# Softplus as one ScalarE function, and a shorter join of float64 words, in an attention and two-MLP kernel

## Chip, cores and metric

The kernel runs on one core of one Trainium2 chip. The metric is the device time of one execution in microseconds (us). TensorE (PE in the profile; PEld is its weight load), VectorE (DVE), ScalarE (ACT), GpSimd (POOL) and the DMA queue that SyncE issues (SP) work beside each other, and each goes through its own instructions in order.

## The reference

Linear attention without softmax, with an RMS norm of each head, feeds an MLP with softplus, and that feeds a second MLP whose hidden layer is the largest of three products:

```python
kv  = einsum('bhsd,bhse->bhde', k, v)              # 8 batches, 8 heads, 576 x 64
o   = einsum('bhsd,bhde->bhse', q, kv)
x   = o / sqrt(mean(o*o) + 1e-6) * g_norm          # 4608 tokens x 512
h   = x @ w_in                                     # 512 x 2048
g   = maximum(h, 0) + log1p(exp(-abs(h)))          # softplus
x   = g @ w_out                                    # 2048 x 512
h   = maximum(maximum(x @ w1, x @ w2), x @ w3)     # 512 x 768 each
out = h @ w_out2                                   # 768 x 512
```

The weights arrive as float64: each is two 32-bit words, which the kernel joins into one float32.

## The kernel before, in words

**Passes.** Features lie on the 128 partitions, tokens run along the free dimension. The 4608 tokens go through in five passes (`NS`): two columns of 464 tokens at a time in passes 0 to 3, two of 448 in pass 4. In every pass the products of the MLPs are 2 x 2 block products by a scheme of seven multiplications: `product` (L309) makes one of seven (`ORDER`), a weight group has seven, and `sums` (L338) collects their results from PSUM: ACT copies (L111) take some out, DVE adds (L120) the others. Groups H0 to H7 make h, X00 to X31 make the second x, then nine groups and an output stage make the second MLP.

**Pass 0** multiplies in float32 (L318), and meanwhile makes the weights. `load_raw` (L209) loads 128 x 512 float64 words into one of two `raw` buffers; `to_f32` (L214) joins them into `sw`, through one PSUM buffer, `cv`: ACT takes the absolute value of the high word (L220), and four DVE operations follow (a lower limit L221, shift and mask L222, sign and top bit L226, the low word's three bits L231). There are two such conversions for each of 25 groups, and six for the output stage, 56 in all. Then POOL makes four sums of a group's weights (`sums_of_weights`, L123 and L120 on POOL), and `make_unit` splits them into a high and a low part for the other passes (ACT cast L111, POOL subtraction L117 into `u`) and writes them to DRAM (`wd`, L165). All of these loads and writes go through SP's one queue.

**Passes 1 to 4** load those parts (`u`, `ux`) and make three fp32r multiplications for each float32 one (`mm3`, L127 to L129). The attention of the next pass runs beside the second MLP of the present one (`attention_beside`).

**The functions touched.** `softplus` (L370) takes one tile of h, 128 x 464: ACT makes |h| (L372), exp (L373), ln (L374), and DVE adds max(h, 0) (L375). A pass has 32 of these, the run 160. `norm` (L499) makes the RMS factor: ACT takes ln (L503), exp (L504) and square (L505), two DVE operations follow (L506, L509), and DVE (L514, pass 0) or POOL (L519) scales the attention's output. There are 40 of these, eight a pass; those of pass 0 come before the first H group. ln, exp and the simple functions stand in one table set, loaded once at the start (L744).

**What sets the order.** Every step of the program is put on a list with a due time (`at`), the list is sorted, and the framework's scheduler then sets each engine's order when the program is built. So a change in a step's operations can move other instructions too.

Of the kernel before, what the change touches and what calls it, by code (L numbers as in the profile page):

```python
# [7 lines left out]
F32 = mybir.dt.float32  # L8
F32R = mybir.dt.float32r
I32 = mybir.dt.int32  # L10
AF = mybir.ActivationFunctionType
ALU = mybir.AluOpType

B, H, S, D = 8, 8, 576, 64
# [11 lines left out]
EPS = 1e-06  # L26

# [13 lines left out]
def kernel(  # L41
# [12 lines left out]
    nc = tc.nc  # L54
# [45 lines left out]
    epsc = const.tile([P, 1], F32, name="epsc")  # L100
# [31 lines left out]
    turns = {}  # L132

    def turn(key, *engs):
        k = turns[key] = turns.get(key, -1) + 1
        return engs[k % len(engs)]
# [16 lines left out]
    wd, units, st = {}, {}, {}  # L153
# [60 lines left out]
    def to_f32(raw, dst):  # L214

        t = psum("cv", "cv")
        lo32, hi32, u = raw[:, :, 0], raw[:, :, 1], t.bitcast(I32)
        nc.scalar.activation(t, hi32.bitcast(F32), AF.Abs)  # L220
        nc.vector.tensor_scalar_max(t, t, 2.0**-15)  # L221
        nc.vector.tensor_scalar(  # L222
            out=u, in0=u, scalar1=3, scalar2=0x3FFFFFF8,
            op0=ALU.logical_shift_left, op1=ALU.bitwise_and,
        )
        nc.vector.scalar_tensor_tensor(  # L226
            out=u, in0=hi32, scalar=-0x40000000, in1=u, op0=ALU.bitwise_and, op1=ALU.bitwise_or
        )
        r = len(dst.shape) - 1
        lo32, u = ((lo32, u) if r == 1 else (a.rearrange("p (i n) -> p i n", i=2) for a in (lo32, u)))  # L230
        nc.vector.scalar_tensor_tensor(  # L231
            out=dst.bitcast(I32), in0=lo32, scalar=29, in1=u,
            op0=ALU.logical_shift_right, op1=ALU.bitwise_or,
        )
# [135 lines left out]
    def softplus(p, src):  # L370
        e = ge_tile(p, "e", src.shape[1])
        nc.scalar.activation(e, src, AF.Abs)  # L372
        nc.scalar.activation(e, e, AF.Exp, scale=-1.0)  # L373
        nc.scalar.activation(e, e, AF.Ln, bias=1.0)  # L374
        nc.vector.scalar_tensor_tensor(  # L375
            out=e, in0=src, scalar=0.0, in1=e, op0=ALU.max, op1=ALU.add
        )
        return e
# [120 lines left out]
    def norm(a, n, p):  # L499

        ss = ss_t.pop((a, p))
        r, t = ctile("r", n), ctile("t", n)
        nc.scalar.activation(r, ss, AF.Ln, scale=1.0 / D, bias=epsc)  # L503
        nc.scalar.activation(r, r, AF.Exp, scale=-0.5)  # L504
# [239 lines left out]
    nc.scalar.preload_act_table_set("natural_log_exp_and_others")  # L744
# [11 lines left out]
    t = -60  # L756
# [103 lines left out]
```

## Time and profile before

| | |
|---|---|
| median of 3 runs | 1477.41 us (1475.75 to 1478.09) |
| profiled execution | span 1475.5 us, first to last instruction; the runs' times stand 0.3 to 2.6 us above it |
| PE busy | 1419.6 us (96%) |
| PEld busy | 1126.5 us (76%) |
| DVE busy | 933.5 us (63%) |
| ACT busy | 835.7 us (57%) |
| POOL busy | 676.5 us (46%) |

Busy is the time with at least one instruction in work; a share over the whole span is an average over stages with different limits. A matmul's end is modelled, and in passes 1 to 4 each overlaps the next, so a short gap between two starts does not show as idle PE; the number of matmuls or weight loads that start in a stretch (the x after a busy time) shows it. Pass 0 with the first attention lasts from 0 to about 400 us, each other pass about 270 us.

### The profile page before, as it was taken

How to read it: one execution, taken by the hardware profiler on the slowest of the kernel's cores; microseconds unless marked ns; L12 is line 12 of the kernel's file. 1: busy time of each engine (PE TensorE's matmuls, PEld its weight loads, DVE VectorE, ACT ScalarE, POOL GpSimd, SP SyncE). 2: the span in 40 equal slices, each digit the busy share in tenths (PEclk: the TensorE clock that was granted, in tenths of full speed). 3: DMA queues.
4: the chain of work that ended last, by engine and by line, in shares of the span. 5: the costliest groups of instructions: out<-in, count | busy, mean ns of one | idle time of the engine just before them, and what ended most of it. 6: DMA issues, size and time to landing. Idle time of an engine off the chain costs nothing.

```text
span 1475.5 us, 18888 instructions
## 1 busy us (share of the span) xinstructions
PE 1419.6 (96%) x6164; PEld 1126.5 (76%) x6164; DVE 933.5 (63%) x1476; ACT 835.7 (57%) x1625; POOL 676.5 (46%) x613
## 2 busy tenths in 40 slices
PE   6799998999999999999999999999999999999999
PEld 4344444555588889788888898888888888998998
DVE  5787888789366676773666656355675545567341
ACT  5676453554187636764866455387636637863321
POOL 3587777633234453451545434433454452445211
PEclk9999999999999999999999999999999999999999
DMA  7758667964366676766566776566676656666562
GB/s 273 251 185 274 214 221 271 337 215 157 110 203 203 217 236 224 266 236 214 190 213 215 247 252 202 167 201 213 212 221 193 215 172 208 206 209 213 183 220 96
DMA packets 107953, 315.56 MB, mean 214 GB/s; under 512 B 12112, under 2 KB 23632, under 8 KB 107856
## 3 DMA queue, kind: packets, MB, share of 16 engines
q1 hardware_dynamic: 107856, 314.36, 65.0%
q8 instruction: 50, 0.82, 0.2%
q14 instruction: 47, 0.39, 0.1%
HBM read 248.78 MB, written 65.54 MB: 213 GB/s over the span
## 4 chain that ended last, share of the span: by engine, by line
PE 74%; DVE 8%; ACT 6%; POOL 4%; issue 4%; DMA 3%; SPq 0%; POOLq 0%; ACTq 0%; DVEq 0%
PE Xx L127 3%; PE Xo L128 3%; PE Xx L129 3%; PE Xx L128 3%; PE Xo L129 3%; PE Xo L127 3%; PE Xh L127 3%; PE Xh L129 3%; PE Xh L128 3%; PE Xo L318 3%; PE oacc L697 3%; PE oacc L128 2%; PE oacc L129 2%; PE oacc L127 2%; PE kvps L412 2%
## 5 line engine op out<-in xcount | busy, mean ns | idle before, releaser
L117 POOL TENSOR_TENSOR lo<-e,hi 128x464 fp32r<-128x464 f32 (+1 forms) x160 | 190.6, 1225 | 197.6 <-ACT hi L111 151.9
L123 POOL TENSOR_TENSOR e<-e 128x464 f32<-128x464 f32 (+1 forms) x40 | 48.2, 1206 | 189.9 <-DVE t L123 164.9
L111 ACT COPY m<-Xo 128x464 f32<-128x464 f32 (+1 forms) x135 | 72.7, 543 | 88.6 <-PE Xo L129 73.7
L111 ACT CAST hi<-t 128x464 fp32r<-128x464 f32 (+1 forms) x96 | 52.1, 544 | 105.0 <-DVE t L123 44.2
L117 POOL TENSOR_TENSOR hl<-m,hh 128x464 fp32r<-128x464 f32 (+1 forms) x48 | 59.0, 1232 | 104.6 <-ACT hh L111 104.6
L375 DVE SCALAR_TENSOR_TENSOR e<-h,e 128x464 f32<-128x464 f32 (+1 forms) x80 | 68.0, 853 | 46.1 <-ACT e L374 45.7
L111 ACT CAST hi<-e 128x464 fp32r<-128x464 f32 (+1 forms) x160 | 87.0, 576 | 16.1 <-PE Yx L128 14.0
L374 ACT ACTIVATE e<-e 128x464 f32<-128x464 f32 (+1 forms) x160 | 92.8, 587 | 2.7
L373 ACT ACTIVATE e<-e 128x464 f32<-128x464 f32 (+1 forms) x160 | 92.9, 588 | 2.4
L120 DVE TENSOR_TENSOR x<-x,Xx 128x464 f32<-128x464 f32 (+1 forms) x120 | 75.3, 628 | 28.3 <-PE Xx L129 26.2
L117 POOL TENSOR_TENSOR u<-sw,u 128x512 fp32r<-128x512 f32 (+1 forms) x76 | 88.2, 1188 | 8.5 <-ACT u L111 8.4
L127 PE MATMUL Xo<-hi,u 128*128 128x464 f32 (+1 forms) x228 | 86.5, 379 | 1.4 <-ACT m L111 1.4
L123 POOL TENSOR_TENSOR sw<-sw 128x256 f32<-128x256 f32 x75 | 57.3, 764 | 65.9 <-DVE sw L231 44.9
L129 PE MATMUL Xo<-hi,u 128*128 128x464 f32 (+1 forms) x228 | 85.0, 373 | 0.0
L128 PE MATMUL Xo<-lo,u 128*128 128x464 f32 (+1 forms) x228 | 85.0, 373 | 0.0
L220 ACT ACTIVATE cv<-raw 128x512 f32<-128x512 f32 x56 | 35.9, 641 | 84.7 <-DVE sw L231 43.6
L519 POOL TENSOR_TENSOR og<-og,r 128x464 f32<-128x464 f32 (+1 forms) x32 | 41.0, 1280 | 88.7 <-DVE r L509 84.3
L127 PE MATMUL Xh<-hi,u 128*128 128x464 f32 (+1 forms) x194 | 73.4, 378 | 4.7 <-ACT h L111 4.3
L129 PE MATMUL Xh<-hi,u 128*128 128x464 f32 (+1 forms) x194 | 71.9, 371 | 0.0
L111 ACT COPY h<-Xh 128x464 f32<-128x464 f32 (+1 forms) x108 | 57.7, 536 | 24.9 <-PE Xh L129 21.4
L128 PE MATMUL Xh<-lo,u 128*128 128x464 f32 (+1 forms) x194 | 71.8, 370 | 0.0
L127 PE MATMUL Xx<-hi,u 128*128 128x464 f32 (+1 forms) x192 | 71.7, 374 | 0.0
(229 smaller groups left out, 4326.7 us busy)
## 6 DMA issues: line engine op xcount, KB each, us to landing
u<-wd SPq DMA_DIRECT2D x198, 512.0 KB, 4.4
ux<-wd SPq DMA_DIRECT2D x96, 512.0 KB, 3.4
wd<-u SPq DMA_DIRECT2D x79, 512.0 KB, 3.1
u<-wd SPq DMA_DIRECT2D x106, 256.0 KB, 3.8
raw<-in_w_out_dram SPq DMA_DIRECT2D x22, 512.0 KB, 4.2
k<-in_kp_dram SPq DMA_DIRECT2D x32, 320.0 KB, 4.9
v<-in_vp_dram SPq DMA_DIRECT2D x32, 320.0 KB, 5.3
raw<-in_w_dram SPq DMA_DIRECT2D x18, 512.0 KB, 4.2
```

The costliest lines, as they stand in the source:

```text
L111: nc.scalar.copy(hi, src)
L117: eng_lo.tensor_tensor(out=lo, in0=src, in1=hi.bitcast(F32), op=ALU.subtract)
L120: eng.tensor_tensor(out=o, in0=a, in1=b, op=ALU.add)
L123: eng.tensor_tensor(out=o, in0=a, in1=b, op=ALU.subtract)
L127: nc.tensor.matmul(acc, wh, xh, start=first, stop=False, skip_group_check=on)
L128: nc.tensor.matmul(acc, wh, xl, start=False, stop=False, skip_group_check=on)
L129: nc.tensor.matmul(acc, wl, xh, start=False, stop=last, skip_group_check=on)
L318: nc.tensor.matmul(acc, w[:, c * P:(c + 1) * P], rhs[m, c], start=first and c == 0, stop=c == 1, skip_group_check=not first)
L373: nc.scalar.activation(e, e, AF.Exp, scale=-1.0)
L374: nc.scalar.activation(e, e, AF.Ln, bias=1.0)
L375: nc.vector.scalar_tensor_tensor(out=e, in0=src, scalar=0.0, in1=e, op0=ALU.max, op1=ALU.add)
L697: nc.tensor.matmul(acc[e, t], w[:, o * P:(o + 1) * P], hh[f, t], start=f == 0, stop=f == NF2 - 1)
```

## The change

Three edits:

- `softplus` is one ACT operation, with the function Softplus. The two other ACT operations and the DVE operation go.
- Softplus is in another table set than ln and exp. `with_table` loads a set when the next function needs another than the last one, and ties the order: a load is issued after all activations that used the set before, an activation after its load. The load at the start goes; the first norm loads its set.
- `to_f32` joins the words with two ACT and two DVE operations. ACT scales the high word, read as float32, by 2^-112 into `cv`, and turns the low word into an integer of its three top bits, in place in `raw`. DVE shifts and joins the two, and then sets the sign from the high word.

```diff
+SLACK = 2.0**-16
+LOW_SCALE = 2.0**-29 * (1 - SLACK)
+LOW_BIAS = -0.5 + 7.5 * SLACK
+NORM_SET, PLUS_SET = "natural_log_exp_and_others", "softplus"
...
+    tables = {"set": None, "load": None, "used": []}
+
+    def after(ins):
+        st = ExitStack()
+        for i in ins:
+            st.enter_context(tc.issue_after(i))
+        return st
+
+    def with_table(name, out, src, func, **kw):
+
+        if tables["set"] != name:
+            with after(tables["used"]):
+                load = nc.scalar.preload_act_table_set(name)
+            tables.update(set=name, load=load.ins, used=[])
+        with after([tables["load"]]):
+            tables["used"].append(nc.scalar.activation(out, src, func, **kw).ins)
...
         lo32, hi32, u = raw[:, :, 0], raw[:, :, 1], t.bitcast(I32)
-        nc.scalar.activation(t, hi32.bitcast(F32), AF.Abs)
-        nc.vector.tensor_scalar_max(t, t, 2.0**-15)
-        nc.vector.tensor_scalar(
-            out=u, in0=u, scalar1=3, scalar2=0x3FFFFFF8,
-            op0=ALU.logical_shift_left, op1=ALU.bitwise_and,
-        )
+        nc.scalar.activation(t, hi32.bitcast(F32), AF.Copy, scale=2.0**-112)
+        nc.scalar.activation(lo32, lo32.bitcast(U32), AF.Copy, scale=LOW_SCALE, bias=LOW_BIAS)
         nc.vector.scalar_tensor_tensor(
-            out=u, in0=hi32, scalar=-0x40000000, in1=u, op0=ALU.bitwise_and, op1=ALU.bitwise_or
+            out=u, in0=u, scalar=3, in1=lo32, op0=ALU.logical_shift_left, op1=ALU.bitwise_or
         )
...
         nc.vector.scalar_tensor_tensor(
-            out=dst.bitcast(I32), in0=lo32, scalar=29, in1=u,
-            op0=ALU.logical_shift_right, op1=ALU.bitwise_or,
+            out=dst.bitcast(I32), in0=hi32, scalar=-0x80000000, in1=u,
+            op0=ALU.bitwise_and, op1=ALU.bitwise_or,
         )
...
     def softplus(p, src):
         e = ge_tile(p, "e", src.shape[1])
-        nc.scalar.activation(e, src, AF.Abs)
-        nc.scalar.activation(e, e, AF.Exp, scale=-1.0)
-        nc.scalar.activation(e, e, AF.Ln, bias=1.0)
-        nc.vector.scalar_tensor_tensor(
-            out=e, in0=src, scalar=0.0, in1=e, op0=ALU.max, op1=ALU.add
-        )
+        with_table(PLUS_SET, e, src, AF.Softplus)
         return e
...
-        nc.scalar.activation(r, ss, AF.Ln, scale=1.0 / D, bias=epsc)
-        nc.scalar.activation(r, r, AF.Exp, scale=-0.5)
+        with_table(NORM_SET, r, ss, AF.Ln, scale=1.0 / D, bias=epsc)
+        with_table(NORM_SET, r, r, AF.Exp, scale=-0.5)
...
-    nc.scalar.preload_act_table_set("natural_log_exp_and_others")
```

The built program has ten table loads where there was one: one at ACT's start, as before, one after the last norm before each pass's softplus (five), and one after the last softplus of each pass but the fifth (four).

ACT at the end of pass 0's attention: the last norm's instructions and the first H group's (`r`, `t` are the norm's tiles, `h11` an evicted product, `e` a softplus), before:

```order
L503 ACTIVATE r_339<-ss_337,epsc_82 128x464
L504 ACTIVATE r_339<-r_339 128x464
L505 ACTIVATE t_340<-r_339 128x464
L220 ACTIVATE cv_477<-raw_411 128x512
L111 COPY h11_400<-Xh_397 128x464
L372 ACTIVATE e_435<-Wh_431 128x464
L373 ACTIVATE e_435<-e_435 128x464
L374 ACTIVATE e_435<-e_435 128x464
```

The same place with the change:

```order
L152 ACTIVATE r_339<-ss_337,epsc_82 128x464
L152 ACTIVATE r_339<-r_339 128x464
L149 ACT_TABLE_LOAD
L512 ACTIVATE t_340<-r_339 128x464
L116 COPY h11_397<-Xh_394 128x464
L236 ACTIVATE cv_517<-raw_445 128x512
L237 ACTIVATE raw_445<-raw_445 128x512
L152 ACTIVATE e_431<-Wh_427 128x464
```

The table load stands between the norm's exp and its square, and the first softplus is one instruction.

ACT in pass 2, where H2 and H3 are evicted and the first four tiles of g are split for X00 (`CAST hi`), before:

```order
L111 COPY h22_5839<-Xh_5742 128x464
L111 CAST hi_5713<-e_5619 128x464
L372 ACTIVATE e_5828<-Wh_5820 128x464
L111 CAST hi_5717<-e_5690 128x464
L373 ACTIVATE e_5828<-e_5828 128x464
L111 CAST hi_5721<-e_5532 128x464
L374 ACTIVATE e_5828<-e_5828 128x464
L111 CAST hi_5725<-e_5575 128x464
L372 ACTIVATE e_5842<-h22_5839 128x464
L373 ACTIVATE e_5842<-e_5842 128x464
L374 ACTIVATE e_5842<-e_5842 128x464
L111 COPY h11_5854<-Xh_5847 128x464
```

The same place with the change:

```order
L116 CAST hi_5464<-e_5329 128x464
L152 ACTIVATE e_5561<-Wh_5553 128x464
L116 CAST hi_5519<-e_5406 128x464
L116 COPY h22_5569<-Xh_5478 128x464
L116 CAST hi_5523<-t1_5525 128x464
L116 COPY h11_5581<-Xh_5574 128x464
L152 ACTIVATE e_5572<-h22_5569 128x464
```

The eviction of H3's first product (`h11`) has one softplus operation between itself and the eviction of H2's last (`h22`) where it had six.

SP's queue in pass 0, where the eleventh to fourteenth load of raw words stand among the writes of the fourth and fifth group's parts (`wd12` to `wd19`), before:

```order
L165 DMA wd13_684<-u_681 128x1024
L211 DMA raw_637<-in_w_out_dram 128x1024
L165 DMA wd14_700<-u_697 128x1024
L165 DMA wd15_714<-u3_711 128x512
L211 DMA raw_675<-in_w_out_dram 128x1024
L165 DMA wd16_753<-u_750 128x1024
L211 DMA raw_731<-in_w_in_dram 128x1024
L165 DMA wd17_778<-u_775 128x1024
L165 DMA wd18_794<-u_791 128x1024
L211 DMA raw_769<-in_w_in_dram 128x1024
L165 DMA wd19_803<-u3_800 128x512
```

The same place with the change:

```order
L181 DMA wd14_658<-u_655 128x1024
L181 DMA wd15_669<-u3_666 128x512
L227 DMA raw_602<-in_w_out_dram 128x1024
L227 DMA raw_636<-in_w_out_dram 128x1024
L181 DMA wd16_701<-u_698 128x1024
L181 DMA wd17_725<-u_722 128x1024
L181 DMA wd18_738<-u_735 128x1024
L181 DMA wd19_747<-u3_744 128x512
L227 DMA raw_682<-in_w_in_dram 128x1024
L227 DMA raw_716<-in_w_in_dram 128x1024
```

The raw loads stand in pairs behind all four writes of a group, where each stood among them.

## Rows read from the trace of the kernel before

**Rows 1.** Windows: PE, PEld, DVE, ACT, POOL busy (x instructions), clock, DMA, GB/s

```profile
0.00:50.00 50.00, 32.58 (x137) 21.41 (x138) 29.56 (x51) 28.01 (x57) 22.26 (x37) 0.97 0.81 279
50.00:300.00 250.00, 231.00 (x646) 114.48 (x645) 202.84 (x312) 140.16 (x273) 176.24 (x177) 0.99 0.71 247
...
400.00:1475.50 1075.50, 1056.05 (x5108) 939.48 (x5106) 628.58 (x999) 624.27 (x1215) 442.53 (x364) 1.00 0.65 209
```

**Rows 2.** Windows, same columns: H and X groups of passes 1 to 4

```profile
425.00:450.00 25.00, 23.01 (x104) 18.65 (x103) 16.73 (x25) 23.24 (x49) 14.06 (x12) 1.00 0.51 174
700.00:725.00 25.00, 23.72 (x108) 19.46 (x107) 15.58 (x28) 23.37 (x48) 15.04 (x13) 1.00 0.59 194
750.00:775.00 25.00, 25.00 (x121) 22.42 (x120) 19.31 (x31) 14.65 (x29) 9.84 (x9) 1.00 0.64 209
975.00:1000.00 25.00, 23.70 (x109) 19.42 (x108) 14.80 (x25) 23.36 (x48) 15.82 (x13) 1.00 0.54 172
1250.00:1275.00 25.00, 23.81 (x112) 20.66 (x113) 17.20 (x30) 20.19 (x43) 11.83 (x11) 1.00 0.62 194
1275.00:1300.00 25.00, 25.00 (x125) 23.17 (x124) 13.89 (x22) 19.99 (x39) 10.94 (x11) 1.00 0.70 221
```

**Rows 3.** Waits of PE, 400 to 1475 us: total us, times, longest

```profile
PE Xh L127 <- ACT h L111: 4.3, 8, 0.9
```

**Rows 4.** Waits of PE, 50 to 300 us

```profile
PE Xx L318 <- DVE x L120: 6.4, 4, 1.9
PE Xh L318 <- ACT h L111: 3.3, 3, 2.1
PE Xh L318 <- DVE og L514: 2.4, 1, 2.4
PE Xx L318 <- ACT x L626: 1.9, 1, 1.9
```

**Rows 5.** Groups of instructions, ACT, 50 to 300 us: busy us, mean ns, idle before

```profile
L220 ACT ACTIVATE cv<-raw 128x512 f32<-128x512 f32 x38 | 24.4, 642 | 66.1 <-DVE sw L231 34.5 <-DMA raw<-in_w_dram 17.8 <-DMA raw<-in_w_out_dram 9.7
L373 ACT ACTIVATE e<-e 128x464 f32<-128x464 f32 x32 | 18.3, 586 | 0.3
```

**Rows 6.** Groups, DVE, 50 to 300 us

```profile
L221 DVE TENSOR_SCALAR cv<-cv 128x512 f32<-128x512 f32 x38 | 26.4, 694 | 19.8 <-ACT cv L220 19.8
L375 DVE SCALAR_TENSOR_TENSOR e<-h,e 128x464 f32<-128x464 f32 x16 | 14.2, 887 | 4.4 <-ACT e L374 4.4
L375 DVE SCALAR_TENSOR_TENSOR e<-Xh,e 128x464 f32<-128x464 f32 x8 | 5.1, 633 | 1.2 <-ACT e L374 1.1
```

**Rows 7.** Windows with L373 (exp of softplus) alone: ACT busy (x)

```profile
700.00:725.00 25.00, 5.02 (x9) 1.00 0.59 194
```

**Rows 8.** DMA issues: KB each, median us from issue to landing

```profile
raw<-in_w_in_dram SPq DMA_DIRECT2D x16, 512.0 KB, 4.7
```

**Rows 9.** Groups, POOL, 50 to 300 us

```profile
L117 POOL TENSOR_TENSOR u<-sw,u 128x512 fp32r<-128x512 f32 x68 | 78.5, 1183 | 4.4 <-ACT u L111 4.4
L123 POOL TENSOR_TENSOR sw<-sw 128x256 f32<-128x256 f32 x57 | 42.2, 740 | 31.1 <-DVE sw L231 23.4 <-PE Yx L318 3.6 <-PE Yo L318 1.2
```

**Rows 10.** Waits of SP's queue, 0 to 300 us: total us, times, longest

```profile
SPq L165 <- POOL u L117: 114.4, 57, 6.8
SPq L211 <- DVE sw L231: 78.4, 29, 6.2
```

**Rows 11.** Timeline of ACT, five places: start us, us, what (idle before, releaser)

```profile
0.73 1.28 ACT L744 ACT_TABLE_LOAD   x1 [0.73 <-PEq L844]
...
518.29 0.58 ACT L374 ACTIVATE e<-e 128x464 f32<-128x464 f32 x1
...
567.17 0.65 ACT L503 ACTIVATE r<-ss,epsc 128x464 f32<-128x464 f32 x1 [1.06 <-PE ss L496]
...
633.80 0.65 ACT L503 ACTIVATE r<-ss,epsc 128x464 f32<-128x464 f32 x1 [1.61 <-PE ss L496]
...
676.19 0.56 ACT L372 ACTIVATE e<-Wh 128x464 f32<-128x464 f32 x1 [1.38 <-DVE Wh L120]
```

More of the change, by code (lines that the diff above doesn't have):

```diff
@@ L10 @@
 I32 = mybir.dt.int32
+U32 = mybir.dt.uint32
 AF = mybir.ActivationFunctionType
@@ L129, in mm3 @@
         nc.tensor.matmul(acc, wl, xh, start=False, stop=last, skip_group_check=on)
[L132 to L136, printed above, removed]
+    tables = {"set": None, "load": None, "used": []}
[11 more added lines that the diff above has]
+            tables["used"].append(nc.scalar.activation(out, src, func, **kw).ins)
     events = []
@@ L219, in to_f32 @@
         lo32, hi32, u = raw[:, :, 0], raw[:, :, 1], t.bitcast(I32)
-        nc.scalar.activation(t, hi32.bitcast(F32), AF.Abs)
-        nc.vector.tensor_scalar_max(t, t, 2.0**-15)
-        nc.vector.tensor_scalar(
-            out=u, in0=u, scalar1=3, scalar2=0x3FFFFFF8,
-            op0=ALU.logical_shift_left, op1=ALU.bitwise_and,
-        )
+        nc.scalar.activation(t, hi32.bitcast(F32), AF.Copy, scale=2.0**-112)
+        nc.scalar.activation(lo32, lo32.bitcast(U32), AF.Copy, scale=LOW_SCALE, bias=LOW_BIAS)
         nc.vector.scalar_tensor_tensor(
-            out=u, in0=hi32, scalar=-0x40000000, in1=u, op0=ALU.bitwise_and, op1=ALU.bitwise_or
+            out=u, in0=u, scalar=3, in1=lo32, op0=ALU.logical_shift_left, op1=ALU.bitwise_or
         )
         r = len(dst.shape) - 1
-        lo32, u = ((lo32, u) if r == 1 else (a.rearrange("p (i n) -> p i n", i=2) for a in (lo32, u)))
+        hi32, u = ((hi32, u) if r == 1 else (a.rearrange("p (i n) -> p i n", i=2) for a in (hi32, u)))
         nc.vector.scalar_tensor_tensor(
-            out=dst.bitcast(I32), in0=lo32, scalar=29, in1=u,
-            op0=ALU.logical_shift_right, op1=ALU.bitwise_or,
+            out=dst.bitcast(I32), in0=hi32, scalar=-0x80000000, in1=u,
+            op0=ALU.bitwise_and, op1=ALU.bitwise_or,
         )
```

## The prediction

> **What bounds the kernel now.** I read the busy time by stretch first, then PE's waits in the stretches where PE is not full, then the groups of instructions that the change touches, and last the queue that feeds pass 0. Most of the run is PE's: from 400 us on it is busy for 1056.1 of 1075.5 us [rows 1]. What the change can give lies in three places.
>
> First, the stretches of passes 1 to 4 in which H groups end and X groups begin. A full stretch of 25 us starts 120 weight loads of 464-token matmuls, or 124 of 448-token ones in pass 4; four stretches start only 103, 107, 108 and 113 [rows 2]. In the first three ACT is busy for 23.2 to 23.4 of 25 us, in the fourth for 20.2. PE waits there for ACT to evict a product (eight waits in all, 4.3 us in the modelled idle time, which hides the short ones) [rows 3]. So ACT is the bound of these stretches, though its share of the run is 57%.
>
> Second, pass 0 from 50 to 300 us. PE is busy for 231.0 of 250 us, and DVE for 202.8 [rows 1]. The four longest sums of PE's 19 us of idle time, 14.0 us together, wait for DVE or ACT [rows 4].
>
> Third, the first 50 us, where PE is busy for 32.6 us [rows 1].
>
> **The change, part by part.** *Softplus.* Per tile two ACT operations of 0.586 us go [rows 5] and one DVE operation of 0.63 us, or 0.89 us where its source is in SBUF [rows 6]. For 160 tiles this is 188 us less on ACT and some 120 us less on DVE. In a stretch such as 700 to 725 us, with ACT at 23.4 us, nine exp stand [rows 7]; 9 x 2 x 0.59 = 10.6 us goes, and ACT is left with some 12.8 of 25 us, below the 15 us of DVE and POOL [rows 2]. The missing weight loads are worth 25 us x (17/120 + 13/120 + 12/120 + 11/124) = 3.5 + 2.7 + 2.5 + 2.2 = 10.9 us. I take four fifths, **8.7 us**, because POOL, at 14 to 16 us of 25 in the first three of these stretches, still makes the low parts in series behind the casts.
>
> No row shows Softplus. The nearest ACT operations of this size take 0.586 us (exp) [rows 5], 0.56 us (absolute value out of PSUM) and 0.65 us (ln with a bias tile) [rows 11]. I take 0.59, between them; the lower end, 0.56, changes nothing that PE waits for. The upper end is two times 0.59, should one instruction do what exp and ln did; it would add 5.3 us to ACT in such a stretch, leave it at 18 us, still under PE, and I put the gain there at half, 5.4 us, for the upper end of the range.
>
> *Joining the words.* Per conversion DVE has four operations, 38 of each between 50 and 300 us, at 0.68 to 0.70 us (L221 stands for all four) [rows 6]. It loses two and keeps two of the same kind; ACT gains one. That is 38 x 1.39 = 53 us less on DVE from 50 to 300 us, and with softplus's 16 x 0.887 + 16 x 0.633 = 24 us the engine goes from 202.8 to some 126 us of 250. ACT there loses 32 x 2 x 0.586 = 37.5 us and gains 38 x 0.64 = 24.4. No row shows an integer source on ACT; the nearest is the 128x512 operation on the same strided words, 0.642 us [rows 5]. I take 0.64. The lower end is that the second operation, which runs beside the first one's DVE step, costs the chain nothing; the upper, twice 0.64, adds 24 us to ACT's 127, which has room. The serial chain through the single PSUM buffer falls from 0.64 + 4 x 0.69 = 3.4 us to 0.64 + 2 x 0.69 = 2.0 us, so a group's two conversions from 6.8 to 4.0 us.
>
> Of the 14.0 us of PE's waits I take half, **7 us**. The rest stays because pass 0 is a loop through the weights too. There are 38 conversions in 250 us, 13.2 us a pair, and PE's own work is 231.0/19 = 12.2 us a pair. The loop has a load of raw words that lands after 4.7 us [rows 8], 4.0 us of conversions, and the waits of in-order engines. POOL's work on a pair's weights, beside it, is over (78.5 + 42.2)/19 = 6.4 us [rows 9]. The order that the scheduler gives SP is less kind than before: both raw loads of a pair now stand behind four writes that wait for POOL. SP already waits 114.4 us for POOL at writes and 78.4 us for DVE at raw loads [rows 10]; ACT sits idle for 27.5 us before L220 until raw words land [rows 5].
>
> *First 50 us.* Some four conversions lie among the norms. Two DVE operations that stood in the norms' way on the longest chain go, and one ACT operation beside them comes: I take 2.2 us less, between nothing and twice that. Against it stands a table load.
>
> *Table loads.* The one load of before takes 1.28 us [rows 11]. Nine more are 11.5 us on ACT. Eight lie where nothing waits. From pass 1's last softplus step at 518 us to the next norm at 567 us there are 48 us, and from the last norm's ln at 634 us to the next softplus at 676 us 41 us [rows 11]; a load there delays that norm's square by 1.28 us while PE has the second MLP's products to do. If that cover were gone, each would cost 1.28 us. The ninth, in pass 0, stands between the last norm's exp and square, and the first MLP waits for that norm (PE waits 2.4 us for `og`) [rows 4]. It costs 1.28 us in full. So the first 50 us give **0.9 us**.
>
> The row shows the load alone, since ACT next waits for PE. The Trainium skill (ScalarE: Activation LUTs, What ACT_TABLE_LOAD costs) states about 2.66 us for a switch, 1.28 us of load and 1.38 us of drain; the row agrees with the first, and no row of before shows the second. By the page the ninth load would cost 1.4 us more and the sum would end at 1462 us.
>
> *Sum.* 8.7 + 7 + 0.9 = 16.6 us, from the profiled execution's span of 1475.5 us to 1458.9 us. The median of the runs stands 1.9 us above that span, so the forecast is 1477.4 - 16.6 = **1460.8 us**.
>
> **The rivals.** (1) *Only ACT's stretches gain.* Pass 0 stays on its weight loop at 13.2 us a pair, since raw loads now come later in SP's queue. For it speak SP's waits [rows 10] and the writes ahead of the raw loads; against it, that a pair's load and conversions come to 8.7 us. Then 8.7 + 0.9 = 9.6 us: 1467.8 us.
>
> (2) *Everything goes.* With DVE at half its time and ACT at half in the four stretches, PE loses nothing there: 10.9 + 14.0 + 2.2, and the clock, 0.99 from 50 to 300 us and 0.97 before [rows 1], comes back with PE's gaps, some 2.5 us. Less than 1.28 for the load, this gives 28.3 us: 1449 us. Against it speaks that other waits usually come next: PE also waits for POOL and for DMAs in these stretches.
>
> (3) *The paired loads stall pass 0: slower.* SP's queue is in order, so a raw load waits until POOL has made the fourth part of a group two before it. If a pair then takes over 13.2 us, pass 0 is slower than before, 19 times. The point from which this decides is 13.2 + 9.6/19 = 13.7 us a pair, where it has eaten what the other places give. At 14.2 us a pair it is 19 us lost, less 9.6: 1487 us. For it speaks the order; against it, that conversions and POOL work on different groups side by side, and that 4.7 + 4.0 us leaves 4.5 us for waits.
>
> (4) *The switches are not hidden.* A set of activations is tied to its load, so if a norm's and a softplus's stretch came to overlap, ACT would stand before each load until the last user of the other set is done. At 1.28 us for each of nine, 11.5 us in place of 1.3, this is 10 us of the gain gone: 1471 us. The order speaks against it: each load stands directly behind the last user of the old set. The Trainium skill (ScalarE: Activation LUTs, Table sets: the hidden batching unit) says to batch activations by set; the order does that, with 32 softplus operations to a load.
>
> (5) *It does not do what it says.* Softplus is as slow as the three operations, or PE's waits at the four stretches go to POOL instead of ACT, and no place gains: 1477 us. POOL at 16 of 25 us speaks against it.
>
> **How the numbers follow.** A measurement of this kernel tells a difference of about 0.2%, 3 us, from none. Chances: the forecast 0.45, rival 1 0.23, rival 2 0.14, rival 3 0.09, rival 4 0.04, rival 5 0.05. Faster by over 0.2% are the forecast and rivals 1, 2 and 4: 0.86. Rival 5 is the same: 0.05. Rival 3 is slower: 0.09. The likeliest case alone has 1454 to 1466 us. The range takes in rivals 1, 2 and 4 with the bounds of Softplus and of the integer operation, 1446 to 1474 us; rivals 3 and 5 are left out.
>
> **What would show it.** Right: ACT at some 13 us in the four stretches, with 118 or more weight loads in each (122 in pass 4); DVE at some 126 us from 50 to 300 us; pass 0 over some 8 us earlier; Softplus at 0.6 us; PE's wait for `og` near 50 us longer by the table load. Wrong: SP's waits for POOL grown and ACT idle before the two word operations until raw words land, with PE waiting for `sw` (rivals 1 and 3); the four stretches still short of loads, with POOL as releaser (rival 5); gaps around the loads of passes 1 to 4 (rival 4).

## The result, and the profile after

The change runs in 1458.91 us (median of four runs, 1454.81 to 1461.59) against 1477.75 us before: a ratio of 0.987, 95% interval 0.9849 to 0.9891, or 18.8 us less. The forecast was 1460.8 us, from a sum of 16.6 us less. The profiled execution of after is the fastest of its runs, with a span of 1453.0 us, 22.5 us under that of before, so the stages below add up to more than the medians differ.

The windows of after that answer to [rows 1], in the same columns (PE, PEld, DVE, ACT, POOL busy, clock, DMA share, GB/s); pass 1 begins 13 us earlier now, so the last row holds a little more of it:

```profile
0.00:50.00 50.00, 32.52 (x128) 20.07 (x128) 25.63 (x42) 32.04 (x64) 22.71 (x38) 0.97 0.79 274
50.00:300.00 250.00, 240.99 (x690) 122.52 (x691) 139.86 (x215) 141.60 (x267) 182.57 (x184) 0.99 0.75 264
...
400.00:1453.00 1053.00, 1038.61 (x5051) 929.08 (x5049) 542.63 (x865) 501.62 (x959) 436.55 (x363) 1.00 0.67 210
```

From 50 to 300 us PE goes from 231.0 to 241.0 us busy, and DVE from 202.8 to 139.9 us. DVE is not at the 126 us that I expected, in part because more of pass 0 falls into the stretch (690 matmul records against 646). ACT hardly moves, 140.2 to 141.6 us: softplus takes some 36 us away there, the join and the table load give back some 29 us, and the rest is the further part of pass 0 that now falls into the stretch.

The stretches where H groups end and X groups begin, of after, as in [rows 2] (the passes begin 13 to 19 us earlier, so a stretch of before lies across two of these):

```profile
400.00:425.00 25.00, 25.00 (x121) 22.31 (x120) 13.35 (x20) 16.73 (x33) 14.82 (x12) 1.00 0.65 204
425.00:450.00 25.00, 25.00 (x121) 22.34 (x120) 10.88 (x18) 14.49 (x29) 12.88 (x11) 1.00 0.70 221
675.00:700.00 25.00, 24.67 (x118) 21.80 (x117) 14.39 (x21) 16.49 (x32) 14.39 (x12) 1.00 0.65 203
700.00:725.00 25.00, 25.00 (x121) 22.38 (x120) 10.89 (x18) 14.13 (x28) 12.91 (x11) 1.00 0.71 220
950.00:975.00 25.00, 24.74 (x118) 21.77 (x117) 12.93 (x20) 16.57 (x32) 14.40 (x12) 1.00 0.67 208
975.00:1000.00 25.00, 25.00 (x121) 22.36 (x120) 10.65 (x18) 14.34 (x29) 12.87 (x11) 1.00 0.65 210
1225.00:1250.00 25.00, 25.00 (x125) 23.16 (x124) 12.81 (x21) 13.78 (x28) 12.72 (x12) 1.00 0.68 205
1250.00:1275.00 25.00, 25.00 (x125) 23.13 (x124) 8.34 (x14) 12.22 (x24) 10.13 (x9) 1.00 0.72 218
```

ACT is at 12 to 17 us of 25 where it was at 20 to 23, and 117 to 120 weight loads start in a stretch (124 in pass 4) where it was 103 to 108 (113). The wait of PE for ACT's evictions in these groups [rows 3] does not appear among the waits after 400 us any more.

PE's waits of after from 50 to 300 us, to set against [rows 4] (total us, times, longest):

```profile
PE Wh L330 <- ACT e L152: 2.3, 1, 2.3
PE kvps L419 <- DMA v<-in_vp_dram: 2.2, 1, 2.2
PE Xo L330 <- ACT m L116: 1.4, 1, 1.4
PE Xh L330 <- ACT h L116: 1.3, 2, 1.1
PE Xx L330 <- DVE x L125: 1.2, 2, 0.6
PE Xh L330 <- DVE t L128: 0.6, 1, 0.6
```

The 14.0 us of the four longest sums of before have become 2.5 us for the same kinds of wait (`Xx` for `x`, `Xh` for `h`); that for `og` now comes before 50 us, with 1.2 us. All of PE's waits in the stretch go from 19.0 to 9.0 us. The longest is new: a PSUM bank (`Wh`) is free only when the first softplus has read it. That softplus stands behind the table load, but run 6 below, which has no load there, has the same wait of 2.3 us, so the load is not shown to be its cause.

SP's waits of after up to 300 us, to set against [rows 10]:

```profile
SPq L181 <- POOL u L122: 113.9, 65, 6.6
SPq L227 <- DVE sw L243: 68.6, 29, 7.4
```

The raw loads stand in pairs now, and yet the queue waits no longer than before.

Groups of ACT from 50 to 300 us of after (busy us, mean ns, idle before), to set against [rows 5]:

```profile
L237 ACT ACTIVATE raw<-raw 128x512 int32<-128x512 uint32 x40 | 26.8, 674 | 21.8 <-DMA raw<-in_w_dram 8.4 <-DMA raw<-in_w_in_dram 6.7 <-DMA raw<-in_w_out_dram 6.6
L236 ACT ACTIVATE cv<-raw 128x512 f32<-128x512 f32 x39 | 25.0, 640 | 32.3 <-DMA raw<-in_w_dram 11.8 <-DVE sw L243 8.1 <-DMA raw<-in_w_out_dram 6.7
L152 ACT ACTIVATE e<-h 128x464 f32<-128x464 f32 x16 | 9.5, 592 | 9.6 <-DVE h L125 9.6
L149 ACT ACT_TABLE_LOAD x1 | 1.3, 1283 | 0.0
```

Softplus takes 592 ns from SBUF, as long as the exp did (586 ns); the integer operation takes 674 ns where I took 640.

### The profile page after: what moved, and what is told of

Read it like the earlier page. It is cut to its first block, busy times and chain, and to the rows that moved or that the text cites. A ratio compares the mean times of both kernels' runs of the same rounds, so it can differ in the third digit from the quotient of the medians.

```text
span 1453.0 us, 18314 instructions
## 1 busy us (share of the span) xinstructions
PE 1412.1 (97%) x6164; PEld 1126.8 (78%) x6164; DVE 761.4 (52%) x1204; ACT 719.6 (50%) x1370; POOL 671.7 (46%) x613
## 4 chain that ended last, share of the span: by engine, by line
PE 83%; DMA 5%; DVE 4%; ACT 3%; issue 2%; POOL 2%; SPq 0%; ACTq 0%; POOLq 0%; DVEq 0%
PE Xh L132 4%; PE Xx L134 4%; PE Xx L132 4%; PE Xx L133 4%; PE Xh L134 4%; PE Xh L133 4%; PE Xo L133 3%; PE Xo L132 3%; PE Xo L134 3%; PE Xo L330 3%; PE Xh L330 3%; PE oacc L704 3%; PE oacc L133 3%; PE oacc L134 2%; PE oacc L132 2%
## 5 line engine op out<-in xcount | busy, mean ns | idle before, releaser
L122 POOL TENSOR_TENSOR lo<-e,hi 128x464 fp32r<-128x464 f32 (+1 forms) x160 | 187.4, 1202 | 216.8 <-ACT hi L116 213.3
L116 ACT CAST hi<-e 128x464 fp32r<-128x464 f32 (+1 forms) x160 | 85.7, 578 | 21.9 <-PE Yx L133 18.7
L152 ACT ACTIVATE e<-h 128x464 f32<-128x464 f32 (+1 forms) x80 | 47.3, 591 | 82.5 <-DVE h L125 81.9
L125 DVE TENSOR_TENSOR h<-h,Yh 128x464 f32<-128x464 f32 (+1 forms) x80 | 50.6, 633 | 52.7 <-ACT h L116 25.0
L125 DVE TENSOR_TENSOR Wh<-h,Wh 128x464 f32<-128x464 f32 (+1 forms) x40 | 25.7, 642 | 93.5 <-PE Wh L134 67.1
L122 DVE TENSOR_TENSOR lo<-t,hi 128x464 fp32r<-128x464 f32 (+1 forms) x96 | 60.4, 633 | 22.0 <-ACT hi L116 20.8
```

The costliest lines, as they stand in the source:

```text
L116: nc.scalar.copy(hi, src)
L122: eng_lo.tensor_tensor(out=lo, in0=src, in1=hi.bitcast(F32), op=ALU.subtract)
L125: eng.tensor_tensor(out=o, in0=a, in1=b, op=ALU.add)
L152: tables["used"].append(nc.scalar.activation(out, src, func, **kw).ins)
```

## The experiments

Every kernel's stages are read off two marks that all of them have: the first DVE addition that completes a product of an H group in a pass, and the eighth, last one. Timeline rows of DVE (start us, us, what) with the first mark of pass 1, before and then after:

```profile
406.56 0.65 DVE L120 TENSOR_TENSOR Wh<-h,Wh 128x464 f32<-128x464 f32 x1 [0.63 <-PE Wh L129]
```

```profile
393.77 0.65 DVE L125 TENSOR_TENSOR Wh<-h,Wh 128x464 f32<-128x464 f32 x1 [0.62 <-PE Wh L134]
```

The table has, for one profiled execution of each kernel, when pass 1 begins by that mark, the time from there to the end, the time from pass 0's first mark to pass 1's ("pass 0"), and the time from first to eighth mark summed over passes 1 to 4 ("H groups"); then the ratio of the timed runs to before with its interval.

| kernel | pass 1 begins, us | from there to the end | pass 0 | H groups, passes 1 to 4 | ratio, 95% interval |
|---|---|---|---|---|---|
| before | 406.6 | 1068.9 | 355.2 | 417.7 | |
| the change | 393.8 | 1059.2 | 343.0 | 408.5 | 0.987 (0.9849 to 0.9891) |
| 1 softplus alone | 400.7 | 1057.5 | 348.1 | 408.7 | 0.9892 (0.9877 to 0.9906) |
| 2 join alone | 413.5 | 1067.3 | 359.8 | 417.7 | 1.0048 (1.0036 to 1.0061) |
| 3 softplus in passes 1 to 4 | 407.5 | 1061.2 | 354.8 | 409.5 | 0.9962 (0.995 to 0.9973) |
| 4 two table loads | 397.7 | 1063.6 | 343.7 | 409.2 | 0.9917 (0.9904 to 0.993) |
| 5 less ACT | 408.9 | 1062.1 | 356.5 | 407.0 | 0.9975 (0.9966 to 0.9983) |
| 6 less DVE | 400.3 | 1061.9 | 347.2 | 412.0 | 0.9919 (0.9906 to 0.9933) |
| 7 three raw buffers | 403.2 | 1059.7 | 343.8 | 409.2 | 0.9916 (0.9903 to 0.993) |
| 8 join, one ACT + three DVE | 405.7 | 1068.3 | 352.1 | 417.6 | 0.9992 (0.9983 to 1.0001) |
| 9 the change with 8's join | 395.0 | 1059.3 | 342.4 | 409.8 | 0.9866 (0.9851 to 0.9881) |
| 10 load behind the square | 394.4 | 1059.2 | 338.3 | 409.5 | 0.9866 (0.9846 to 0.9887) |
| 11 9 and 10 together | 396.7 | 1059.5 | 344.5 | 409.5 | 0.9874 (0.9858 to 0.9889) |
| 12 DVE operation off the chain | 411.7 | 1066.4 | 360.2 | 417.6 | 1.005 (1.0034 to 1.0066) |

The column of the H groups is steady: 417.6 or 417.7 us in every kernel with the old softplus there, 408.5 to 409.8 us in every one with the new. When pass 1 begins is less so: the scheduler makes another order for each edit, and the change's own runs lie 6.8 us apart. The start differs too: pass 0's first mark lies between 50.7 and 59.4 us. From 0 to 50 us TensorE's granted clock, a mean over its two levels (2.4 and 1.2 GHz), is 0.97 before and with the change, 0.93 in runs 1, 6 and 8, and 0.90 in runs 2 and 9; PE is busy for 32 to 34 of these 50 us in all of them. The column "pass 0" leaves that start out.

**1. Softplus alone.** The change, with the old five operations in `to_f32` (both versions stand in the diff above).

> The change without its join of words: Softplus and the tied table loads, the old five operations per conversion. Theory (ACT's relief pays in passes 1 to 4, the shorter join and the relief together pay in pass 0): passes 1 to 4 gain all of the change's 9.7 us, as in the change's trace, pass 0 gains some 4 of its 12.8 us, ratio to before near 0.991 (13 us). Rival (the join is needed everywhere, since what it frees reaches the later passes): under 5 us. Rival (softplus pays for all, the join for nothing): 0.987, pass 1 begins 12 us earlier.

Measured: 0.9892. Pass 1 begins 5.9 us earlier, and the rest is 11.4 us shorter. The theory holds for the later passes: they have their whole gain from softplus alone. For pass 0 this run is not softplus alone. The old join's absolute value stands on ACT between softplus operations, and the trace has a table load before it and one before the next softplus. There are 48 loads in place of the change's ten; 36 of the 38 others fall into the stretch from 50 to 300 us:

```profile
L236 ACT ACT_TABLE_LOAD x18 | 23.1, 1283 | 0.5
L152 ACT ACT_TABLE_LOAD x18 | 23.1, 1283 | 0.3
```

L236 is the absolute value here, L152 the helper of softplus and norm. ACT is busy for 162.9 us in this stretch, against 140.2 before, and pass 0 is still 7.1 us shorter. In the change the join has a scaled copy in place of the absolute value, and no load stands before it. How much of pass 0's further 5.1 us (343.0 against 348.1) is due to these loads, and not to the shorter join, no run separates.

**2. The join alone.** Before, with the two new ACT operations and the two DVE operations in `to_f32`.

> The change's join of words alone, with the old softplus and one table load. Theory: nothing in passes 1 to 4, where nothing is joined; pass 0 gains some 7 us through DVE's relief and the shorter chain: ratio 0.995, pass 1 begins near 394 us in place of 401. Rival (SP's paired raw loads hold pass 0): no gain, 1.000, or slower. The two parts add up to the change's 22 us in spans if they are independent.

Measured: 1.0048, slower by 7 us. Nothing in the later passes, as expected (H groups 417.7), but pass 1 begins 6.9 us later, not 7 us earlier. The theory was off. The rival had the right direction, but its reason does not show: SP's two waits of [rows 10] come to 189.9 us up to 300 us, against 192.8 before. Windows and ACT's two groups from 50 to 300 us of this kernel:

```profile
50.00:300.00 250.00, 226.13 (x627) 110.66 (x627) 150.42 (x230) 158.19 (x306) 179.02 (x177) 0.99 0.70 249
```

```profile
L225 ACT ACTIVATE raw<-raw 128x512 int32<-128x512 uint32 x36 | 24.2, 674 | 21.5 <-DMA raw<-in_w_dram 11.5 <-DMA raw<-in_w_out_dram 5.6 <-DMA raw<-in_w_in_dram 4.4
L224 ACT ACTIVATE cv<-raw 128x512 f32<-128x512 f32 x37 | 23.3, 631 | 14.9 <-DMA raw<-in_w_dram 7.8 <-DMA raw<-in_w_out_dram 4.1 <-DVE sw L231 3.0
```

DVE has 52 us less to do than before, and PE still loses 5 us. ACT has 18 us more, and waits for raw words in front of both operations, with evictions and softplus's three operations queued behind. These waits are hardly longer than before (33.4 us, against 31.3 in front of L220, of which [rows 5] lists 27.5); what is new is the operation. Two of PE's waits in this stretch:

```profile
PE Xh L318 <- ACT h L115: 5.4, 4, 3.3
PE Xx L318 <- DVE e L375: 2.5, 2, 1.3
```

The first, for evictions, was 3.3 us [rows 4]; the second, for the end of softplus, was not there. The two parts of the change do not add up: by the timed ratios 16 us less (run 1) and 7 us more make 19 us less when they come together. Run 1's further table loads, which only the old join brings, may be a part of that difference.

**3. Softplus in passes 1 to 4 only**, with the old join; pass 0 keeps the three operations:

```diff
+        if p:
+            with_table(PLUS_SET, e, src, AF.Softplus)
+        else:
+            nc.scalar.activation(e, src, AF.Abs)
...
```

> Softplus as one function in passes 1 to 4 alone, the old three operations in pass 0 and the old join. Theory: pass 1 begins where it did before (401 us, within 2), and the four later passes are 9 to 10 us shorter in all: ratio 0.9935. Rival (part of the later passes' gain comes from pass 0's order, for instance from weights written earlier): under 6 us, above 0.996.

Measured: 0.9962 (6.8 us by the medians). Its profile has pass 1 at 407.5 us, one later than before, and the rest 7.7 us shorter, 8.2 us of it in the H groups. The stages follow the theory, at four fifths of its size; the median alone would fit the rival's line. The H groups say which: they gain about the same (8.2 us, against 9.2 with the change) whether pass 0 is changed or not.

**4. Two table loads at each switch.**

```diff
+                load = nc.scalar.preload_act_table_set(NORM_SET if name == PLUS_SET else PLUS_SET)
+            with after([load.ins]):
                 load = nc.scalar.preload_act_table_set(name)
```

> The change with two table loads at each of its ten switches (the other set's first, then the right one). Theory (only the load between the last norm's exp and its square in pass 0 stands on the chain): 1.3 us slower than the change, and the load at the start is hidden behind the first DMAs; ratio near 0.988. By a drain behind each load, as the Trainium skill (ScalarE: Activation LUTs, What ACT_TABLE_LOAD costs) gives it, 2.7 us: 0.989. Rival (the switches are not hidden): nine times 1.28 us, 11.5 us slower than the change, 0.995.

Measured: 0.9917, between the two: 4.4 us above the change by the medians, 6.9 us by the ratios, 8.3 us by the profiles. Of these 8.3 us, 3.9 lie before pass 1 and 2.6 in pass 2 (274.1 us from its first mark to the next pass's, against 271.5). The load itself is the same 1283 ns. The second load at the start costs nothing that shows: ACT's next instruction begins at 7.99 us, against 7.95. In pass 0 the first load of the switch already begins 3.2 us later than in the change (51.48 us, against 48.25), so the loads of that switch are not what makes the first mark 3.2 us late; from there to pass 1 it takes 343.7 us, against 343.0. So ten more loads are neither free nor all on the chain (10 x 1.28 = 12.8 us). Why pass 2 takes part of it stays open; one execution each does not tell 2.6 us of one stage from scatter.

**5. Less ACT: softplus without exp and ln.** The output has |h| in place of log1p(exp(-|h|)).

```diff
         nc.scalar.activation(e, src, AF.Abs)
-        nc.scalar.activation(e, e, AF.Exp, scale=-1.0)
-        nc.scalar.activation(e, e, AF.Ln, bias=1.0)
```

> The kernel before with two of softplus's three ACT operations left out (exp and ln; the absolute value and the DVE operation stay), so ACT is relieved as by the change and DVE is not; no table switch. The output lacks log1p(exp(-|h|)) and has |h| in its place. Theory (ACT's queue was the bound of the four stretches of passes 1 to 4): those passes gain 8 to 10 us, as with Softplus; pass 0 some 3 us. Ratio 0.992. Rival (DVE's operation at the end of the chain is what is late): under 3 us, above 0.998.

Measured: 0.9975. In the H groups of passes 1 to 4 the theory holds: 407.0 us, 10.7 us less than before and the least of all kernels. But the whole of these passes gains only 6.8 us (1062.1 against 1068.9), under the 8 to 10 expected: what follows the H groups takes 3.9 us longer, and why stays open. Pass 0 gains nothing (pass 1 begins 2.3 us later), so the ratio missed 0.992. One of the four stretches of this kernel:

```profile
700.00:725.00 25.00, 25.00 (x121) 22.39 (x120) 18.68 (x28) 16.05 (x33) 15.87 (x13) 1.00 0.67 217
```

ACT is at 16 us and 120 weight loads start, with DVE at 18.7 us, 3 us more than in this stretch before.

**6. Less DVE: softplus without its DVE operation.** The output lacks max(h, 0).

```diff
         nc.scalar.activation(e, e, AF.Ln, bias=1.0)
-        nc.vector.scalar_tensor_tensor(
-            out=e, in0=src, scalar=0.0, in1=e, op0=ALU.max, op1=ALU.add
-        )
```

> The kernel before with softplus's DVE operation left out (max(h,0) is not added), all three ACT operations kept: DVE is relieved, ACT is not. Theory: passes 1 to 4 gain under 3 us, since the evictions still stand behind three ACT operations per tile; pass 0 gains some 2 to 4 us. Ratio 0.997. Rival (DVE is what is late): 8 to 10 us in passes 1 to 4, 0.991.

Measured: 0.9919, by the number the rival's 0.991 and not the theory's 0.997; but pass 0 has a large part in it. Passes 1 to 4 gain 7.0 us, 5.7 of it in the H groups: more than the theory's 3, less than the rival's 8, and in the H groups half of what ACT's relief gives. The same stretch, and then the one that answers to it when both are counted from pass 2's first mark, which comes 8.9 us earlier here:

```profile
700.00:725.00 25.00, 24.68 (x117) 21.48 (x116) 12.59 (x22) 20.70 (x44) 11.40 (x11) 1.00 0.62 200
691.10:716.10 25.00, 24.21 (x114) 20.71 (x113) 10.57 (x18) 23.82 (x51) 15.28 (x13) 1.00 0.58 193
```

In the second, ACT is as full as before (23.8 of 25 us, against 23.4), DVE is busy for less than half of it, and 113 weight loads start, against 107 before and 120 in a full stretch. So with DVE relieved it is still ACT that is full there, and about half of the loss stays. From 50 to 300 us the windows of this kernel are:

```profile
50.00:300.00 250.00, 236.39 (x672) 118.78 (x671) 185.76 (x289) 148.09 (x286) 175.79 (x179) 0.99 0.74 257
```

PE is busy for 5.4 us more than before there, and pass 1 begins 6.3 us earlier, as early as with the whole of softplus in one function (run 1, 5.9 us). In pass 0 it is leaving out the DVE operation that pays (8.0 us from first mark to first mark), not leaving out the two ACT operations (1.3 us longer in run 5).

**7. Three raw buffers.** `bufs=3` for `raw`, and each raw load due one conversion earlier.

> The change with three buffers of raw words in place of two, and each raw load due one conversion earlier. Theory (pass 0 is still partly held by the loop of raw load, conversion and SP's queue): pass 0 gains 2 to 4 us more than the change, ratio 0.985. Rival (PE bounds pass 0 from 50 us on, 241 of 250 us busy): same as the change within 1.5 us, 0.987.

Measured: 0.9916. Pass 1 begins at 403.2 us, 9.4 us later than in the change, nearly all of it before the first H group: the first mark of pass 0 comes at 59.4 us, against 50.7 us. From there to pass 1 it takes 343.8 us, against 343.0. So from the first H group on the buffers do not hold pass 0, as the rival said; the time as a whole missed both lines because of the start. There the third raw load now goes out at 6.6 us, ahead of the attention's k and v, whose last load of the first 60 us goes out at 20.9 us, against 16.8; PE's wait for the squares of the norm's input (`ss` waits for `sq`) is 12.8 us up to 60 us, against 6.1, and the clock granted from 40 to 60 us is 0.66, against 0.91: more of it at the lower level.

**8. The join in one ACT and three DVE operations**, on the kernel before: the low word stays in the last DVE operation.

```diff
-        nc.scalar.activation(t, hi32.bitcast(F32), AF.Abs)
-        nc.vector.tensor_scalar_max(t, t, 2.0**-15)
+        nc.scalar.activation(t, hi32.bitcast(F32), AF.Copy, scale=2.0**-112)
         nc.vector.tensor_scalar(
-            out=u, in0=u, scalar1=3, scalar2=0x3FFFFFF8,
+            out=u, in0=u, scalar1=3, scalar2=0x7FFFFFF8,
...
-            out=u, in0=hi32, scalar=-0x40000000, in1=u, op0=ALU.bitwise_and, op1=ALU.bitwise_or
+            out=u, in0=hi32, scalar=-0x80000000, in1=u, op0=ALU.bitwise_and, op1=ALU.bitwise_or
```

> The kernel before with a join in one ACT operation (the scaled copy) and three DVE operations (the low word stays in the last one): DVE loses one operation of 0.69 us per conversion, ACT gains none, softplus stays as before. The join alone in two and two was 7 us slower than before. Theory A (its second ACT operation did that: it waits for raw words in ACT's in-order queue, ahead of evictions and softplus's three operations): this one is no slower than before, 0.996 to 1.000, pass 0 from its first H group to pass 1 in 350 to 355 us (before 355.2, join alone 359.8). Theory B (the shorter chain itself did it, through the order that the scheduler makes of it, raw loads paired): slower than before again, 1.002 or more.

Measured: 0.9992, pass 1 0.9 us earlier, and 352.1 us from its first H group to pass 1, within theory A's 350 to 355. It differs from run 2 in that one operation per conversion is DVE's and not ACT's, and it is not slower; so moving that operation to ACT is what made run 2 slow, with whatever order the scheduler makes of it. That ACT's waits for raw words did it, as theory A has it in its brackets, is not shown: they hardly grew in run 2. Nor is it clearly faster, though DVE has 22 us less to do from 50 to 300 us:

```profile
50.00:300.00 250.00, 233.00 (x661) 116.34 (x660) 180.45 (x276) 141.42 (x276) 177.55 (x177) 0.99 0.72 254
```

**9. The change with that join.**

> The change with the join in one ACT and three DVE operations. Theory A (beside the new softplus ACT has room for the second operation, and DVE is what pass 0 wants relieved): 1 to 3 us slower than the change, ratio 0.989, between the change and softplus alone (0.9892). Rival (ACT's waits for raw words cost the change something as well): 2 to 4 us faster than the change, 0.985.

Measured: 0.9866 (1456.30 us), the same as the change within the intervals, with pass 1 at 395.0 us. Neither side shows: beside the new softplus the second ACT operation costs nothing that can be measured, and the DVE operation that it replaces costs nothing either. With runs 2 and 8 this makes a square: moving the operation from DVE to ACT changes the ratio from 0.9992 to 1.0048 with the old softplus, and from 0.9866 to 0.987 with the new. Read the other way, the join of run 8, which brings nothing by itself, and the new softplus together already have the whole gain.

**10. The table load behind the norm's square.**

```diff
-        nc.scalar.activation(t, r, AF.Square, scale=0.125)
+        with_table(NORM_SET, t, r, AF.Square, scale=0.125)
```

> The change with the norm's square tied to the norm's table set, so that each load comes behind the square and not before it. Theory (the load costs 1.28 us on pass 0's chain and is hidden elsewhere): PE's first wait for og near 48 us shorter by up to 1.28 us, ratio 0.986, 1 us better than the change. Rival (the first softplus, two ACT instructions behind, waits for the load just the same): no difference, 0.987.

Measured: 0.9866, pass 1 at 394.4 us: no difference in the whole that can be measured, as the rival said. PE's wait for `og` in the first 56 us is 2.8 us (two waits) against 1.2 us, not shorter. The parts do differ: pass 0's first mark comes at 56.0 us, 5.3 us later than in the change, and from there it takes 4.7 us less. The last norm's exp already begins 3.6 us later, before any load, so this run does not price the one load.

**11. Runs 9 and 10 together**, in search of a better kernel.

> The change with the join in one ACT and three DVE operations and the load behind the norm's square, together. Theory (each was the same as the change within its interval): 0.986, 1 to 2 us better than the change if the two add. Rival (order noise of the scheduler outweighs both): anywhere from 0.984 to 0.990.

Measured: 0.9874 (1457.56 us). They do not add; no version here beats the change by more than the intervals.

**12. The DVE operation of pass 0 off the chain.** As before, but in pass 0 it writes a scratch tile that nobody reads.

```diff
         nc.vector.scalar_tensor_tensor(
-            out=e, in0=src, scalar=0.0, in1=e, op0=ALU.max, op1=ALU.add
+            out=s, in0=src, scalar=0.0, in1=s, op0=ALU.max, op1=ALU.add
         )
```

> The kernel before with softplus's DVE operation in pass 0 kept at its place and size, but written to a scratch tile that nobody reads, so DVE has the same work and the products of g no longer wait for it (the output of pass 0 lacks max(h,0)); passes 1 to 4 as before. Leaving the operation out gained 8 us in pass 0. If its place on the chain was what cost (DVE's queue between ln and the split): pass 0 from its first H group to pass 1 near 347 us, as without it, ratio 0.994. If DVE's busy time was what cost: near 355 us as before, ratio 1.000.

Measured: 1.005, pass 1 at 411.7 us, 5.1 us later than before, and 360.2 us from the first H group. So with the operation off the chain of g the gain of run 6 does not come; that the time is even longer is no more than the scheduler's order has done in other runs. That leaves the operation's time in DVE's queue, or what it holds while it waits its turn (the PSUM bank that it reads). DVE's time in sum does not explain it: from 50 to 300 us DVE is busy for 185.8 us in run 6, which gains 8.0 us in pass 0, and for 180.5 us in run 8, which gains 3.1.

PE's waits tell more. The longest one of before is for DVE's adds of the second x, which free a PSUM bank (6.4 us [rows 4], 1.2 us with the change). The same wait in runs 5, 8 and 12, which keep softplus's DVE operation in pass 0, and in run 6, which does not:

```profile
PE Xx L318 <- DVE x L120: 8.5, 4, 2.9
PE Xx L317 <- DVE x L120: 5.9, 5, 1.6
PE Xx L318 <- DVE x L120: 7.7, 4, 2.8
PE Xx L318 <- DVE x L120: 1.8, 2, 1.1
```

One of these waits of before ends at 162.35 us. DVE's queue has there, a few places ahead of the add that PE waits for, one of softplus's operations, which itself waited for ACT's ln:

```profile
157.00 1.76 DVE L375 SCALAR_TENSOR_TENSOR e<-h,e 128x464 f32<-128x464 f32 x1 [0.65 <-ACT e L374]
161.58 0.62 DVE L120 TENSOR_TENSOR x<-x,Xx 128x464 f32<-128x464 f32 x1
```

No wait of PE for `e` of DVE is on the list of before in this stretch. So the waits point to the operation's place in DVE's queue, ahead of the adds of x, and not to its place on the chain of g or to the bank that it reads. Run 2 keeps the operation and has 1.0 us of this wait, with 52 us less on DVE; there other waits came in its place.

## Why the prediction was right, and where it was not

**The median.** 1458.9 us against 1460.8, with the direction and the size of the gain in the forecast's own range of 1454 to 1466 us. That it came within 1.9 us is in part luck: the terms of the sum come to 16.6 us, the profiled executions differ by 22.5, of which pass 0 has 5.2 us more than its term, for a reason that I did not have; and the medians differ by 18.8.

**ACT's stretches in passes 1 to 4: right.** I said 8.7 us. The H groups of these passes are 9.2 us shorter in the change, and all that follows pass 1's mark 9.7 us. Run 5 bears ACT out as the bound: relieving it alone gives 10.7 us there. Run 6 does so from the other side: with DVE relieved ACT is still busy for 23.8 of 25 us, and weight loads are still missing. It also shows that the DVE operation has a share of its own (5.7 us), which I had not counted. The two together do not add, since there are only some 11 us to be had. What a shorter chain for each tile does, apart from a freer ACT, no run separates: run 5 shortens both. (In the order of pass 2 shown ahead of the prediction, the eviction of H3's first product has no softplus operation between itself and the eviction of H2's last, where the text there says one.)

**Pass 0: right in sign, mis-sized, and with a wrong reason.** I took 7 us, half of PE's waits; from first mark to first mark the change has 12.2 us (355.2 to 343.0). The step that failed is "joining the words": I argued that 53 us less on DVE and a shorter chain free PE, and that ACT "has room" for the second operation. By itself the join costs 7 us (run 2); without its second ACT operation it costs nothing and brings nothing that the timed runs show (run 8). With softplus in one operation, the change has pass 0 in 343.0 us and run 1 in 348.1, and the timed ratios, 0.987 against 0.9892, have intervals that overlap; and what lies between them may be run 1's 38 further table loads, which the new join does without. Which join it is, run 8's or the change's, then makes no difference (run 9, 342.4 us). What pays for itself in pass 0 is that softplus's DVE operation goes (run 6, 8.0 us), of which I counted the busy time only: PE's wait for the adds of x, behind it in DVE's queue, falls from 6.4 to 1.8 us.

**First 50 us: near in size, not shown in its terms.** I said 0.9 us; the first mark of pass 0 is at 50.7 us against 51.3. No run shows the two terms, 2.2 us less for two DVE operations and 1.28 us more for the load: runs 2 and 8, with fewer DVE operations and no load, have that mark at 53.6 us, at a lower granted clock. The sign that I named, a longer wait for `og`, did not come (1.2 us, against 2.4).

**Table loads: right for the eight, open for the ninth.** ACT's timeline of after around the load in pass 0 (start us, us, what):

```profile
47.65 0.59 ACT L152 ACTIVATE r<-r 128x464 f32<-128x464 f32 x1
48.25 1.28 ACT L149 ACT_TABLE_LOAD   x1
49.55 0.59 ACT L512 ACTIVATE t<-r 128x464 f32<-128x464 f32 x1
```

The load begins 0.01 us after the exp ends and the square begins 0.02 us after the load: a switch takes some 1.3 us. The Trainium skill (ScalarE: Activation LUTs, What ACT_TABLE_LOAD costs) adds a drain of 1.38 us, which these rows do not show, so its variant of the sum (1462 us) has no ground here. I put the whole load on the chain in pass 0; that is not shown: the time is the same when the square goes first (run 10), but the start of pass 0 moved by more than a load there.

**The rivals.** The paired raw loads (3) and the weight loop (1) did not come: SP's waits did not grow, and a third buffer changes nothing after the first H group (343.8 against 343.0 us). "Everything goes" (2) was nearer than the forecast by pass 0's marks, which give 12.2 us against 7 and 14.0; PE's idle time from 50 to 300 us fell by 10.0 us, between the two. "The switches are not hidden" (4) is out for the change itself, whose later passes gain as much as in theory; run 4 says that a second load at each switch would not be free. In run 1, where activations of two sets alternate, the loads do come in numbers, 38 more of them. (5) is out: Softplus takes 0.59 us, and 117 to 124 weight loads start in the stretches.

**Open.** Whether the join brings anything in the change beyond sparing table loads: a run with the new softplus and the old join, with a function in place of the absolute value that needs no load, would tell. How softplus's DVE operation cost pass 0 its 8 us is told by PE's waits and not by a run that moves the operation behind the adds of x. And whether the second ACT operation slows run 2 by its 24 us, by its waits for raw words, or by the order that the scheduler makes of it; the waits alone do not, since with the change ACT idles longer for raw words (45.4 us before the two operations, against 33.4). The order moves with every edit, and runs 7 and 12 show that it can cost 5 to 9 us.

## What to carry to other kernels

An engine with a modest share of the whole run can bound a short stretch: count what the busiest engine starts there (weight loads in 25 us), not its modelled busy time. When work moves from one engine to another, ask what is queued behind it at its new place: here one operation more per conversion on ACT, with softplus's three operations and the evictions in the same queue, cost more than the two that it saved on DVE, and the same edit was harmless once that queue was shorter. Time the parts of a change apart and together, since here 16 us less and 7 us more made 19 us less; and read the trace of each part before you add them up, since a part by itself can bring in work that neither kernel has, as run 1 did with its table loads.

## What the runs showed that I had not expected

A table switch costs some 1.3 us with no drain beside the load. With the softplus set in use, an absolute value on ACT got a table load before it, 19 times in run 1, while copy, cast and square went without. A 32-bit integer source on ACT, read and written in place at every second word, costs 674 ns for 128x512 where the float operation on the same words costs 640 ns.
